# Pooled attention followed by eight experts on one core: chunk counts and weight maxima in the experts' PSUM banks as soon as they are ready, more slots for the weight loads, lists filled behind the first keys

## The chip, the cores and the metric

The kernel runs on one core of a Trainium2 chip. The metric is the device time of one execution in microseconds; the time before is the median of three runs. The engines are named as in the profile: PE (TensorE matmul), PEld (its weight loads), DVE (VectorE), ACT (ScalarE), POOL (GpSimd), SP (SyncE, which here only issues DMAs).

## The reference, cut to what matters

Four batches of 12288 queries attend to 768 keys each (keys and values are the same, a 4x4 mean pool of kv times a 128x128 matrix). The 49152 result rows are the tokens of a mixture of eight experts: each token goes to the one expert with the largest gate logit.

```python
kv_pool = kv.reshape(B, H // r, r, W // r, r, C).mean(axis=(2, 4))
k = v = kv_pool.reshape(B, -1, C) @ w_sr                  # 4 x 768 x 128
a = softmax(scale * (q @ k.transpose(0, 2, 1)))
x = (a @ v).reshape(B * S, D)                             # 49152 x 128
...
logits = x @ w_gate; e_idx = np.argmax(logits, axis=1)
gate_w = softmax(logits)[np.arange(N), e_idx]; eom = sigmoid(x @ w_output_gate)
for e in range(E):
    h = np.maximum(x[mask] @ w1[e], 0.0)                  # w1: 128 x 1024
    out[mask] = gate_w[mask, None] * eom[mask, e, None] * (h @ w2[e])
```

## The kernel before

**Work.** Float32 operands are split into two float16 halves, so each product is three float16 matmuls. 512 queries are a *group* (96 of them, number i); four groups are a *chunk* (24, number c). Nearly all tokens of a chunk have the same favourite expert, so the whole chunk is run through that expert, and the few other tokens are scattered to lists in DRAM (`scr`) and computed at the end, 128 per tile.

**Order of the work.** The main loop steps over i = 0 to 104, and each step over eight *slots* s. In a slot the work of several groups stands side by side: scores and softmax of group i (`qk`, on even slots, block j = s/2), value products of group i-1 (`pv`, in slot 5), gate logits of group i-2, and from i = 8 on (`MOE_LAG`) the expert of group i-8 (`moe_h`, `moe_y`: one block f of 128 hidden units per slot). PE, POOL and SP run exactly in the order in which this loop writes the instructions; DVE and ACT are ordered by the scheduler, which may pull an instruction ahead of earlier written ones. `with behind():` ties a DVE instruction behind the latest one that was marked (`mark["dve"]`: the score maximum or the latest `HL`).

**One slot of the expert.** PE makes H (three matmuls), ACT writes HH = relu(H) in float16, DVE writes HL = max(H,0) - HH, PE uses HH and HL for Y some slots later. H, the value product U, the logits `lg` and their transposes `lT` share one ring of three PSUM banks, `psH`: a new tile waits until the third last one has been read by ACT and DVE. Scores S have their own ring of two double banks, `psA`; columns 384 to 511 of each bank are free beside S's 384 columns.

**Routing.** When the logits of a chunk are there (step 4c+5), `routing(c)` runs as a generator, one stage per slot: maximum, one-hot (`oh`), sums per partition (`oh16`), then two small matmuls that count each expert's tokens in all and before each partition, then the favourite expert `ei`, then the indices, and 16 indirect DMAs on POOL that write `scr`. Before, the two count matmuls are put on a list `hooks`; the next `qk` with j in `HJ` (0 or 1; for the first steps not before (7, 0), `H0`) takes them off and writes the result into the free columns of its S.

**Weights.** `w_load(c)` reads `ei` on SP and loads the favourite's w1 and w2 (512 KB each). For the first six chunks (`NDW`) the float32 weights are then halved here by `w_split`, begun `WD` slots after the load: `w_power` takes the largest magnitude (four DVE reductions of 128x512), turns it round with two PE transposes (through `hooks` again, except c = 0), and gets a power of two; then ACT, DVE and POOL write the halves. From step `BK0` on, every `BKD` steps, `w_bank(e)` does the same for one of the eight experts, `BKW` slots after its load, and writes the halves to DRAM (`wbank`), where chunks 6 to 23 load them ready made.

**Lists.** `fill` sets the lists' 3.3 MB to a neutral row. Before, it begins at step 8 and issues one of eight DMAs every third slot (`FS`); a scatter waits until all are issued (`FILLED`).

Of the kernel before, what the change touches and what calls it, by code (L numbers as in the profile page):

```python
# [53 lines left out]
class Cfg:  # L54
# [12 lines left out]
    R3 = 2  # L67
    RG = 1
    RSEQ = (1, 2, 1, 1)
    FS = 3  # L70
    HJ = (0, 1)
    H0 = (7, 0)
    LC = 4
    WD = 4
    NDW = 6
    BK0, BKD, BKW = 11, 2, 8
    WT = 1
    QL, QT, QN = 0, 2, 6
    QP0, QPA = 4, 3
# [9 lines left out]
def body(ctx, tc, q, kv, w_sr, w_gate, w_og, w1, w2, out, cfg=Cfg):  # L89
# [61 lines left out]
    def largest(m, ps):  # L151

        dve.tensor_reduce(out=m, in_=ps, op=ALU.max, axis=AX.X)
        dve.tensor_scalar(m, m, 2.0 ** -100, None, op0=ALU.max)
# [195 lines left out]
        dve.tensor_tensor(qf[:, 1, :], ps, qf[:, 0, :], op=ALU.subtract)  # L350
        QS[i] = qT

    hooks = []
    spare = {"n": 0}

    def qk(i, j):

        K2 = KVT[i // GPB][0]
        KH, KL = K2[:, 0, :], K2[:, 1, :]
        c, g = divmod(i, CG)  # L360
        es = QM[c][:, 2, g:g + 1]
        if j == 0:
            PTt[i] = wk.tile([P, 2 * NKB, GT], F16, tag="PT", bufs=2, name=f"PT{i}")
            if g == 0:
                SUMS[c] = rt.tile([P, CB], F32, tag="SUM", bufs=4, name=f"SUM{c}")
        S = psA.tile([P, 2, 512], F32, tag="A", name=f"S{i}_{j}")
        if hooks and (j in cfg.HJ if i >= MOE_LAG else (i, j) >= cfg.H0):
            hooks.pop()(S)
        m = i - MOE_LAG - 1
        scale = moe_turn(m, j - 2, S) if j >= 2 and m >= 0 else None  # L370
        qh, ql = QS[i][:, j, :], QS[i][:, GB + j, :]
        for h in range(2):
            pe.matmul(S[:, h, 0:384], qh, KH[:, ts(h, 384)], start=True, stop=False)  # L373
        for h in range(2):
            pe.matmul(S[:, h, 0:384], qh, KL[:, ts(h, 384)], start=False, stop=False)  # L375
        for h in range(2):
            pe.matmul(S[:, h, 0:384], ql, KH[:, ts(h, 384)], start=False, stop=True)  # L377
        nm = wk.tile([P, 2], F32, tag="nm", bufs=4, name=f"nm{i}_{j}")
        with after(mark.get("nm")):
            dve.tensor_reduce(out=nm[:, 0:1], in_=S[:, :, 0:384], op=ALU.max, axis=AX.XY, negate=True)  # L380
# [3 lines left out]
        act.activation(pr.rearrange("p (a k) -> p a k", a=2), S[:, :, 0:384], AF.Exp,  # L384
                       bias=nm[:, 1:2], scale=es, accum_out=SUMS[c][:, bl:bl + 1])
# [87 lines left out]
    def routing(c):  # L473
# [27 lines left out]
        with nc.allow_low_precision("counts up to CB"):  # L501
            dve.tensor_reduce(out=oh16, in_=ohT, op=ALU.add, axis=AX.X)
        yield
        ps = []

        def counts(S):
            pe.matmul(S[:, 0, 384:384 + E], ones16, oh16, start=True, stop=True)
            pe.matmul(S[:, 1, 384:384 + E], tri16, oh16, start=True, stop=True)
            ps.append(S)

        if c == NCK - 1:
            for _ in range(cfg.LC):
                yield
            counts(psA.tile([P, 2, 512], F32, tag="A", name=f"cps{c}"))
        else:
            hooks.append(counts)
        while not ps:
            yield
        cnt = T("cnt", [P, 2, E])
        dve.tensor_copy(cnt, ps[0][:, :, 384:384 + E])  # L520
        yield
        cm = T("cm", [P, 4])
        dve.tensor_reduce(out=cm[:, 0:1], in_=cnt[:, 0, :], op=ALU.max, axis=AX.X)
# [56 lines left out]
        for n, t0, b in ((1, tok0, CT * c), (2, row0, 2 * CT * c), (3, row0, 2 * CT * c + GB)):  # L580
            pool.tensor_scalar(rw[:, :, n:n + 1], t0.unsqueeze(2), 1.0, float(b), op0=ALU.mult, op1=ALU.add)
        yield
        while not FILLED:
            yield
        SCT.add(c)
        for bl in range(CB):
            spare["n"] += 1
# [31 lines left out]
                     in_=w2[e, :, :].rearrange("o (k p) d -> p (o k) d", p=P))  # L619
        return t  # L620

    def w_power(t, nm, hook, x=""):

        m = kvp.tile([P, 8], F32, tag="wm" + x, name=f"wm{nm}")
        m4 = kvp.tile([P, 2, 2], F32, tag="wm4" + x, name=f"wm4{nm}")
        mb = kvp.tile([P, 2, P], F32, tag="wmb" + x, bufs=1, name=f"wmb{nm}")
        for y in range(2):
            for n in range(2):
                dve.tensor_reduce(out=m4[:, y, n:n + 1], in_=t[:, n, ts(y, 512)], op=ALU.max, axis=AX.X,
                                  apply_absolute_value=True)  # L630
            yield
        dve.tensor_tensor(m[:, 0:2], m4[:, 0, :], m4[:, 1, :], op=ALU.max)
        dve.tensor_copy(mb, m[:, 0:2].unsqueeze(2).to_broadcast([P, 2, P]))
        for _ in range(cfg.WT):
            yield
        ps = []

        def turn(S):
            for n in range(2):
                pe.transpose(S[:, n, 384:512], mb[:, n, :], ident)  # L640
            ps.append(S)

        if hook:
            hooks.append(turn)
        else:
            turn(psA.tile([P, 2, 512], F32, tag="A", name=f"wps{nm}"))
        while not ps:
            yield
        largest(m[:, 0:2], ps[0][:, :, 384:512])
# [27 lines left out]
    def w_bank(e):  # L677
# [83 lines left out]
    def fill():  # L761

        f = wk.tile([P, FR, RW], F32, tag="o", name="fill")
        pool.memset(f, 0.0)
        pool.memset(f[:, :, 1:2], BIG)
        pool.memset(f[:, :, 3:4], float(GB))
        yield
        for e in range(E):
            sp.dma_start(out=scr[e * REG:(e + 1) * REG, :].rearrange("(p a b) r -> p a (b r)", p=P, b=FR),
                         in_=f.rearrange("p b r -> p (b r)").unsqueeze(1).to_broadcast([P, REG // P // FR, FR * RW]))  # L770
# [122 lines left out]
    with tc.manual_schedule(engines={pool.engine, sp.engine, pe.engine}):  # L893
# [44 lines left out]
        for i in range(NG + MOE_LAG + 1):  # L938
# [140 lines left out]
```

## Time and profile before

| | |
|---|---|
| median of three runs | 2064.8 us (2062.18 to 2068.03) |
| profiled execution, time | 2063.95 us |
| its span (first to last instruction) | 2062.2 us |
| PE busy | 1916.5 us, 93% |
| DVE busy | 1608.1 us, 78% |
| ACT busy | 1381.6 us, 67% |
| POOL busy | 1156.2 us, 56% |
| mean granted TensorE clock | 0.989 |

Besides the page, the profile is read through views: a table of busy times by stretch of time, a list of who waited for whom, and the instructions in order of time. A time in these views counts from the span's first instruction. In a row of the table by stretch the numbers are: the stretch, its length, then busy us and count for PE, PEld, DVE, ACT and POOL, the granted clock, the DMA share and GB/s. In a row of the instructions in order of time they are: start, duration, engine, line, operation, and in brackets the idle time before it and what ended it. Step i begins with the first matmul of S for group i, j = 0; by that, step 8 begins at 132.4 us, 11 at 195.6, 15 at 289.5, 19 at 384.9, 23 at 477.4, 27 at 571.8, 31 at 660.4, and steps 41 to 44 last from 862.6 to 940.9.

### The profile page before, as it was taken

The numbers are of one execution on the slowest core, as the hardware profiler recorded it, in microseconds if no ns is written. First come the engines' busy times: TensorE is split into PE (matmuls) and PEld (weight loads), VectorE is DVE, ScalarE is ACT, GpSimd is POOL, SyncE is SP. The second block draws the span as 40 slices with busy tenths as digits, with TensorE's granted clock in tenths as the row PEclk, the third lists the DMA queues.
The fourth block names the chain that finished last, engine by engine and source line by source line (L and its number), as shares of the span: only waits on it lengthen the run. The fifth ranks groups of instructions, "written<-read, shape, count | busy, mean of one in ns | idle before, by whom it ended". The sixth has DMA issues, their size and how long they took to land. (4 is left out here: it accounts for less than half of the span.)

```text
span 2062.2 us, 30671 instructions
## 1 busy us (share of the span) xinstructions
PE 1916.5 (93%) x9789; PEld 976.6 (47%) x9789; DVE 1608.1 (78%) x3296; ACT 1381.6 (67%) x2470; POOL 1156.2 (56%) x995
## 2 busy tenths in 40 slices
PE   4878989798999999999999999999999999999997
PEld 2544444343444544444544544445445445445444
DVE  6788798988878778788687687787787787786673
ACT  3766767676767676776777766776776776776653
POOL 1543667666566765654656756645645645646531
PEclk9989999999999999999999999999999999999999
DMA  6979989888897887888889997977977977877712
GB/s 182 179 153 248 218 205 220 196 176 190 185 206 178 186 189 154 163 157 165 163 185 200 186 193 135 179 166 141 184 158 144 179 160 152 172 153 147 144 54 66
DMA packets 898898, 351.07 MB, mean 170 GB/s; under 512 B 822240, under 2 KB 840801, under 8 KB 898736
## 3 DMA queue, kind: packets, MB, share of 16 engines
q1 hardware_dynamic: 885824, 348.63, 81.1%
q0 software_dynamic: 12480, 0.40, 0.5%
q8 instruction: 78, 1.28, 0.3%
q14 instruction: 84, 0.69, 0.1%
q10 hardware_dynamic: 432, 0.07, 0.0%
HBM read 86.19 MB, written 62.91 MB: 72 GB/s over the span
## 5 line engine op out<-in xcount | busy, mean ns | idle before, releaser
L391 POOL TENSOR_TENSOR ph<-pr,ph 128x768 f16<-128x768 f32 x384 | 632.3, 1647 | 709.6 <-ACT ph L390 424.0
L711 DVE SCALAR_TENSOR_TENSOR HL<-H,HH 128x512 f16<-128x512 f32 x768 | 526.3, 686 | 115.8 <-ACT HH L710 103.2
L710 ACT ACTIVATE HH<-H 128x512 f16<-128x512 f32 x768 | 452.4, 590 | 213.9 <-PE H L707 211.0
L384 ACT ACTIVATE pr<-S,nm,qm 128x768 f32<-128x768 f32 x384 | 380.3, 990 | 202.3 <-DVE nm L381 163.5
L588 POOL DMA_INDIRECT scr<-rw,idx x384 | 384.3, 1001 | 93.8 <-issue 80.8
L418 PE MATMUL U<-PT,V 128*128 128x512 f16 (+1 forms) x1854 | 393.4, 367 | 33.1 <-DVE HL L711 27.9
L380 DVE TENSOR_REDUCE nm<-S 128x1 f32<-128x768 f32 x384 | 364.7, 950 | 49.8 <-PE S L377 49.2
L705 PE MATMUL H<-U,w 128*128 128x512 f16 x768 | 293.0, 381 | 31.5 <-DVE U L423 15.1
L390 ACT ACTIVATE ph<-pr 128x768 f16<-128x768 f32 x368 | 309.3, 840 | 3.6 <-issue 2.1
L721 PE MATMUL Y<-HH,w 128*128 128x512 f16 x768 | 292.3, 381 | 4.7 <-ACT ys L726 4.0
L418 PEld LDWEIGHTS <-V 128*128 128x128 f16 x1854 | 181.5, 98 | 238.8 <-issue 45.6
L723 PE MATMUL Y<-HL,w 128*128 128x512 f16 x768 | 292.2, 381 | 2.3 <-DVE HL L711 2.3
L706 PE MATMUL H<-U,w 128*128 128x512 f16 x768 | 292.8, 381 | 0.0
L707 PE MATMUL H<-U,w 128*128 128x512 f16 x768 | 292.8, 381 | 0.0
L722 PE MATMUL Y<-HH,w 128*128 128x512 f16 x768 | 292.1, 380 | 0.0
L373 PE MATMUL S<-K,qT 128*128 128x384 f16 x768 | 189.5, 329 | 9.9 <-ACT pr L384 4.7
L375 PE MATMUL S<-K,qT 128*128 128x384 f16 x768 | 189.5, 329 | 0.0
L377 PE MATMUL S<-K,qT 128*128 128x384 f16 x768 | 189.4, 329 | 0.0
L423 DVE SCALAR_TENSOR_TENSOR U<-U,U 128x512 f16<-128x512 f32 x96 | 64.8, 675 | 127.1 <-ACT U L422 127.1
L422 ACT ACTIVATE U<-U 128x512 f16<-128x512 f32 x96 | 56.8, 592 | 120.4 <-PE U L418 120.3
L706 PEld LDWEIGHTS <-w 128*128 128x128 f16 x768 | 75.3, 98 | 104.2 <-issue 42.3
L722 PEld LDWEIGHTS <-w 128*128 128x128 f16 x768 | 75.3, 98 | 96.5 <-issue 10.3
(222 smaller groups left out, 2185.2 us busy)
## 6 DMA issues: line engine op xcount, KB each, us to landing
kvs<-in_kv_dram SPq DMA_DIRECT2D x96, 256.0 KB
q<-in_q_dram SPq DMA_DIRECT2D x96, 256.0 KB
urows<-uT SPq DMA_DIRECT2D x96, 256.0 KB
out_dram<-o SPq DMA_DIRECT2D x96, 256.0 KB
w<-wbank SPq DMA_DIRECT2D x36, 512.0 KB
wb<-in_moe_w_dram SPq DMA_DIRECT2D x16, 512.0 KB
wbank<-wbo SPq DMA_DIRECT2D x16, 512.0 KB
PT<-ph SPq DMA_TRANSPOSE x384
```

The costliest lines, as they stand in the source:

```text
L380: dve.tensor_reduce(out=nm[:, 0:1], in_=S[:, :, 0:384], op=ALU.max, axis=AX.XY, negate=True)
L384: act.activation(pr.rearrange("p (a k) -> p a k", a=2), S[:, :, 0:384], AF.Exp, bias=nm[:, 1:2], scale=es, accum_out=SUMS[c][:, bl:bl + 1])
L390: act.activation(ph[:, 0, :], pr, AF.Copy)
L391: pool.tensor_tensor(ph[:, 1, :], pr, ph[:, 0, :], op=ALU.subtract)
L418: pe.matmul(PVP[i][:, cols], ops[n][0], ops[n][1][:, cols], start=(n == 0), stop=(n == len(ops) - 1))
L588: ins = pool.indirect_dma_start(out=scr, out_offset=bass.IndirectOffsetOnAxis(ap=idx[:, bl:bl + 1], axis=0), in_=rw[:, bl, :], in_offset=None,
L705: pe.matmul(H, w1h[:, ts(f, P)], UH, start=True, stop=False)
L706: pe.matmul(H, w1h[:, ts(f, P)], UL, start=False, stop=False)
L707: pe.matmul(H, w1l[:, ts(f, P)], UH, start=False, stop=True)
L710: act.activation(HH, H, AF.Relu)
L711: mark["dve"] = dve.scalar_tensor_tensor(HL, H, 0.0, HH, op0=ALU.max, op1=ALU.subtract)
L722: pe.matmul(Y, w2l[:, ts(f, P)], HH, start=False, stop=False)
```

## The change

Five things are changed together.

1. The two count matmuls and the transposes of the weights' maxima no longer go through `hooks` into the free columns of S. They take a bank of the ring `psH`, and are issued one slot after `oh16` (counts), `WT` = 1 slot after the maxima (chunk weights) or `BKT` = 3 slots after them (experts' bank).
2. The four reductions of `w_power` are one per slot instead of two, and each is tied `behind()` the latest marked DVE instruction.
3. `w_split` begins six slots after its load instead of four (`WD`).
4. The experts' banks begin at step 9 instead of 11 (`BK0`), and wait 14 slots instead of 8 for their loads (`BKW`).
5. `fill` is issued at once behind the first keys' and the first three query loads, and no scatter waits for it any more.

```diff
-    FS = 3
-    HJ = (0, 1)
-    H0 = (7, 0)
     LC = 4
-    WD = 4
+    WD = 6
     NDW = 6
-    BK0, BKD, BKW = 11, 2, 8
+    BK0, BKD = 9, 2
+    BKW, BKT = 14, 3
...
     def qk(i, j):
...
-        if hooks and (j in cfg.HJ if i >= MOE_LAG else (i, j) >= cfg.H0):
-            hooks.pop()(S)
...
     def routing(c):
...
-        def counts(S):
-            pe.matmul(S[:, 0, 384:384 + E], ones16, oh16, start=True, stop=True)
-            pe.matmul(S[:, 1, 384:384 + E], tri16, oh16, start=True, stop=True)
-            ps.append(S)
-
-        if c == NCK - 1:
-            for _ in range(cfg.LC):
-                yield
-            counts(psA.tile([P, 2, 512], F32, tag="A", name=f"cps{c}"))
-        else:
-            hooks.append(counts)
-        while not ps:
+        for _ in range(cfg.LC if c == NCK - 1 else 1):
             yield
+        ps = psH.tile([P, GT], F32, tag="H", name=f"cps{c}")
+        pe.matmul(ps[:, 0:E], ones16, oh16, start=True, stop=True)
+        pe.matmul(ps[:, E:2 * E], tri16, oh16, start=True, stop=True)
         cnt = T("cnt", [P, 2, E])
...
-        while not FILLED:
-            yield
         SCT.add(c)
...
     def w_power(t, nm, wt, x=""):
...
-        for y in range(2):
-            for n in range(2):
-                dve.tensor_reduce(out=m4[:, y, n:n + 1], in_=t[:, n, ts(y, 512)], op=ALU.max, ...)
-            yield
+        for n in range(2):
+            for y in range(2):
+                with behind():
+                    dve.tensor_reduce(out=m4[:, y, n:n + 1], in_=t[:, n, ts(y, 512)], op=ALU.max, ...)
+                yield
...
-        for _ in range(cfg.WT):
+        for _ in range(wt):
             yield
...
+        ps = psH.tile([P, GT], F32, tag="H", name=f"wps{nm}")
+        for n in range(2):
+            pe.transpose(ps[:, ts(n, P)], mb[:, n, :], ident)
+        largest(m[:, 0:2], ps[:, 0:2 * P].rearrange("p (n x) -> p n x", n=2))
+        yield
...
         for i in (1, 2):
             q_load(i)
+        fill()
         q_power(0, 0, 1)
```

**What stands where, before and after.** In the rows below a name carries the group or chunk and then the block (S41_3 is block 3 of group 41's scores, HL33_6 block 6 of group 33's hidden units), with the tile's running number behind it. Lines are those of the kernel before and of the changed one, each in its own count.

SP at the first weight load: `ei0` is read from SBUF (TENSOR_LOAD), then chunk 0's two weight tensors (`wr0`) are loaded; `PT` are the transposes of the probabilities. Before:

```order
L401 DMA_TRANSPOSE PT7_1142<-ph7_0_1157 128x12x128
L334 DMA_TRANSPOSE qT9_1196<-q29_1193 128x8x128
L604 TENSOR_LOAD ei0_1172
L604 ISA x2
L617 ISA
L617 DMA wr0_1207<-in_moe_w1_dram 128x1024
L618 ISA
L618 DMA wr0_1207<-in_moe_w2_dram 128x8x128
L401 DMA_TRANSPOSE PT7_1142<-ph7_1_1186 128x12x128
```

After:

```order
L396 DMA_TRANSPOSE PT5_883<-ph5_3_1005 128x12x128
L291 DMA q12_1061<-in_q_dram 128x512
L587 TENSOR_LOAD ei0_1040
L587 ISA x2
L600 ISA
L600 DMA wr0_1072<-in_moe_w1_dram 128x1024
L601 ISA
L601 DMA wr0_1072<-in_moe_w2_dram 128x8x128
L396 DMA_TRANSPOSE PT6_1042<-ph6_0_1055 128x12x128
```

The load has moved up by a little over one step: it stands ahead of group 6's first transpose instead of behind group 7's first.

DVE at the end of step 10 and the start of step 11: `wm41` are the four reductions of chunk 1's weights, `wm4b0` those of expert 0's bank, `U29` the value product of group 9, `nm` score maxima. Before:

```order
L741 TENSOR_TENSOR o1_1938<-S10_2_1937,msw0_1346 128x256
L629 TENSOR_REDUCE wm41_2042<-wr1_1904 128x1 x2
L332 SCALAR_TENSOR_TENSOR q215_2661<-q15_1578,qm3_1160,q215_2661 128x512
L629 TENSOR_REDUCE wm41_2042<-wr1_1904 128x1 x2
L423 SCALAR_TENSOR_TENSOR U29_2001<-U9_1982,U29_2001 128x512
L380 TENSOR_REDUCE nm10_3_2021<-S10_3_2012 128x1
L711 SCALAR_TENSOR_TENSOR HL2_6_2035<-H2_6_2030,HH2_6_2034 128x512
```

After:

```order
L716 TENSOR_TENSOR o1_2013<-S10_2_2012,msw0_1341 128x256
L686 SCALAR_TENSOR_TENSOR HL2_5_2052<-H2_5_2047,HH2_5_2051 128x512
L613 TENSOR_REDUCE wm41_2084<-wr1_1875 128x1
L330 SCALAR_TENSOR_TENSOR q215_2746<-q15_1633,qm3_1244,q215_2746 128x512
L418 SCALAR_TENSOR_TENSOR U29_2077<-U9_2058,U29_2077 128x512
L375 TENSOR_REDUCE nm10_3_2099<-S10_3_2090 128x1
L376 TENSOR_SCALAR nm10_3_2099<-nm10_3_2099,qm2_652 128x1
L686 SCALAR_TENSOR_TENSOR HL2_6_2113<-H2_6_2108,HH2_6_2112 128x512
L613 TENSOR_REDUCE wm41_2084<-wr1_1875 128x1
L716 TENSOR_TENSOR o1_2013<-S10_3_2090,msw0_1341 128x256
L686 SCALAR_TENSOR_TENSOR HL2_7_2128<-H2_7_2123,HH2_7_2127 128x512
L613 TENSOR_REDUCE wm4b0_2136<-wb0_1637 128x1
```

One reduction instead of four stands ahead of `U29`; the others are spread between the `HL`.

DVE at the end of step 41, where PE has written the value product U40 and S41_3 (`scl9`, `cnt9` to `x19` are routing of chunk 9). Before:

```order
L541 SCALAR_TENSOR_TENSOR z9_10170<-z9_10170,sume9_9919 128x16
L542 SCALAR_TENSOR_TENSOR z9_10170<-se9_10166,z9_10170 128x16
L544 RECIPROCAL scl9_10189<-z9_10170 128x16
L423 SCALAR_TENSOR_TENSOR U240_10013<-U40_9994,U240_10013 128x512
L380 TENSOR_REDUCE nm41_3_10026<-S41_3_10017 128x1
L381 TENSOR_SCALAR nm41_3_10026<-nm41_3_10026,qm10_8405 128x1
L711 SCALAR_TENSOR_TENSOR HL33_6_10040<-H33_6_10035,HH33_6_10039 128x512
L741 TENSOR_TENSOR o32_9952<-S41_3_10017,msc8_9229 128x256
```

After:

```order
L529 RECIPROCAL scl9_10148<-z9_10109 128x16
L505 COPY cnt9_10042<-cps9_10039 128x16
L508 TENSOR_REDUCE cm9_10073<-cnt9_10042 128x1
L549 SCALAR_TENSOR_TENSOR st9_10210<-cnt9_10042,ebase_101 128x8
L510 SCALAR_TENSOR_TENSOR ce9_10075<-cnt9_10042,cm9_10073,w8_95 128x8
L551 TENSOR_TENSOR x19_10212<-x09_10174,st9_10210 128x128
L418 SCALAR_TENSOR_TENSOR U240_10035<-U40_10016,U240_10035 128x512
L375 TENSOR_REDUCE nm41_3_10053<-S41_3_10044 128x1
L511 TENSOR_REDUCE cm9_10073<-ce9_10075 128x1
L552 TENSOR_TENSOR x19_10212<-x19_10212,oh9_9969 128x128
L376 TENSOR_SCALAR nm41_3_10053<-nm41_3_10053,qm10_8435 128x1
L686 SCALAR_TENSOR_TENSOR HL33_6_10067<-H33_6_10062,HH33_6_10066 128x512
```

Before, the counts' followers come behind `nm42_0` and `HL34_0` in step 42; now the first five of them stand ahead of `U240`. On PE the two count matmuls stand between U40 and S41_3 (before: ahead of S42_0), and in the ring `psH` their tile stands between U40 and H33_6, so that H33_7 now takes the bank of U40, which H34_0 took before.

More of the change, by code (lines that the diff above doesn't have):

```diff
@@ L351, in q_prep @@
         QS[i] = qT
-    hooks = []
     spare = {"n": 0}
@@ L503, in routing @@
         yield
-        ps = []
-        def counts(S):
-            pe.matmul(S[:, 0, 384:384 + E], ones16, oh16, start=True, stop=True)
-            pe.matmul(S[:, 1, 384:384 + E], tri16, oh16, start=True, stop=True)
-            ps.append(S)
-        if c == NCK - 1:
-            for _ in range(cfg.LC):
-                yield
-            counts(psA.tile([P, 2, 512], F32, tag="A", name=f"cps{c}"))
-        else:
-            hooks.append(counts)
-        while not ps:
+        for _ in range(cfg.LC if c == NCK - 1 else 1):
             yield
+        ps = psH.tile([P, GT], F32, tag="H", name=f"cps{c}")
+        pe.matmul(ps[:, 0:E], ones16, oh16, start=True, stop=True)
+        pe.matmul(ps[:, E:2 * E], tri16, oh16, start=True, stop=True)
         cnt = T("cnt", [P, 2, E])
-        dve.tensor_copy(cnt, ps[0][:, :, 384:384 + E])
+        dve.tensor_copy(cnt, ps[:, 0:2 * E].rearrange("p (x e) -> p x e", x=2))
         yield
@@ L620, in w_raw, with w_power @@
         return t
-    def w_power(t, nm, hook, x=""):
+    def w_power(t, nm, wt, x=""):
         m = kvp.tile([P, 8], F32, tag="wm" + x, name=f"wm{nm}")
@@ L626, in w_power @@
         mb = kvp.tile([P, 2, P], F32, tag="wmb" + x, bufs=1, name=f"wmb{nm}")
-        for y in range(2):
-            for n in range(2):
-                dve.tensor_reduce(out=m4[:, y, n:n + 1], in_=t[:, n, ts(y, 512)], op=ALU.max, axis=AX.X,
-                                  apply_absolute_value=True)
-            yield
+        for n in range(2):
+            for y in range(2):
+                with behind():
+                    dve.tensor_reduce(out=m4[:, y, n:n + 1], in_=t[:, n, ts(y, 512)], op=ALU.max, axis=AX.X,
+                                      apply_absolute_value=True)
+                yield
         dve.tensor_tensor(m[:, 0:2], m4[:, 0, :], m4[:, 1, :], op=ALU.max)
         dve.tensor_copy(mb, m[:, 0:2].unsqueeze(2).to_broadcast([P, 2, P]))
-        for _ in range(cfg.WT):
+        for _ in range(wt):
             yield
[L636 to L649, printed above, removed]
+        ps = psH.tile([P, GT], F32, tag="H", name=f"wps{nm}")
[3 more added lines that the diff above has]
+        yield
         powers(m[:, 2:4], m[:, 4:6], m[:, 0:2])
@@ L655, in w_split @@
         t = WT[c]
-        m = yield from w_power(t, f"{c}", att and c)
+        m = yield from w_power(t, f"{c}", cfg.WT)
         MSC[c] = msc = rt.tile([P, CB], F32, tag="msw", bufs=4, name=f"msw{c}")
@@ L685, in w_bank @@
             yield
-        m = yield from w_power(t, f"b{e}", True, "_b")
+        m = yield from w_power(t, f"b{e}", cfg.BKT, "_b")
         dve.tensor_copy(fac[:, e:e + 1], m[:, 6:7])
@@ L766, in fill @@
         pool.memset(f[:, :, 3:4], float(GB))
-        yield
         for e in range(E):
@@ L770, in fill @@
                          in_=f.rearrange("p b r -> p (b r)").unsqueeze(1).to_broadcast([P, REG // P // FR, FR * RW]))
-            yield
-        FILLED.append(True)
-    FILLED = []
     def tail_prep():
@@ L909, in body @@
         tix, tgen = [], []
-        filler, begun = None, False
+        begun = False
         bk, nbk = [], 0
@@ L946, in body @@
                 rc = None
-            if i == MOE_LAG:
-                filler = fill()
             for s in range(8):
-                if filler and (8 * i + s) % cfg.FS == 0 and next(filler, 1) == 1:
-                    filler = None
                 if s == 0 and 0 <= ri < NG:
```

## The prediction

> **What bounds the kernel now.** I read the page first: which engine is full, and in which part of the span it is not.
>
> ```profile
> PE 1916.5 (93%) x9789; PEld 976.6 (47%) x9789; DVE 1608.1 (78%) x3296; ACT 1381.6 (67%) x2470; POOL 1156.2 (56%) x995
> PE   4878989798999999999999999999999999999997
> DVE  6788798988878778788687687787787787786673
> ```
>
> PE is the bound, and from the eleventh slice on (516 us) it stays at nine tenths or more. Most of its missing 146 us (2062.2 - 1916.5) lie ahead of that. So the table by stretch came second, cut where groups 8, 11, 15, 19, 23 and 27 begin, with one late chunk (steps 41 to 44) as the measure.
>
> ```profile
> 132.40:195.60 63.20, 60.45 (x290) 28.99 (x289) 48.08 (x103) 40.22 (x71) 22.27 (x18) 0.93 0.90 198
> 195.60:289.50 93.90, 83.73 (x407) 41.31 (x406) 76.77 (x154) 64.33 (x116) 59.95 (x50) 0.95 1.04 236
> 289.50:384.90 95.40, 81.65 (x409) 40.83 (x408) 82.86 (x165) 64.44 (x116) 65.11 (x57) 0.98 0.88 197
> 384.90:477.40 92.50, 80.62 (x409) 40.41 (x407) 79.19 (x172) 64.93 (x117) 60.10 (x53) 1.00 0.85 185
> 477.40:571.80 94.40, 82.97 (x403) 40.35 (x401) 80.62 (x171) 64.18 (x113) 52.23 (x44) 0.96 0.87 185
> 571.80:660.40 88.60, 81.13 (x402) 40.26 (x400) 74.55 (x147) 62.31 (x113) 58.56 (x50) 0.98 0.87 193
> 862.60:940.90 78.30, 77.19 (x395) 38.96 (x394) 61.53 (x123) 55.16 (x99) 42.89 (x36) 1.00 0.86 162
> ```
>
> Four steps cost 78.3 us late and 92.5 to 95.4 us in the four stretches from 195.6 to 571.8, which hold the experts' banks and the chunks' own weights: 376.2 us against 313.2, 63 us lost, and 10.3 more in the stretch behind. DVE does 76.8 to 82.9 us there against 61.5 late, so it is nearly a second bound. Third came the list of waits from 132 to 660 us, and in it those of PE, and of DVE and ACT for a DMA.
>
> ```profile
> PE H L705 <- DVE U L423: 15.1, 6, 4.6
> PE H L705 <- DVE HL L711: 13.4, 18, 2.0
> PE U L418 <- DVE HL L711: 12.8, 8, 2.8
> PE wps L640 <- DVE wmb L633: 9.3, 1, 9.3
> DVE wm4b L629 <- DMA wb<-in_moe_w_dram: 9.0, 6, 4.1
> DVE wm L629 <- DMA wr<-in_moe_w_dram: 4.1, 4, 1.8
> ACT q L331 <- DMA qT<-q: 7.9, 2, 4.6
> ```
>
> PE waits 41.3 us for banks of `psH` that DVE has not yet read (15.1+13.4+12.8), and DVE in turn stands 13.1 us before weights that have not landed. How the two hang together is seen in order of time:
>
> ```profile
> 194.76 0.43 DVE L741 TENSOR_TENSOR o<-S,msw 128x256 f32<-128x256 f32 x1 [4.54 <-ACT pr L384]
> 196.81 1.28 DVE L629 TENSOR_REDUCE wm<-wr 128x1 f32<-128x512 f32 x2 [1.62 <-DMA wr<-in_moe_w_dram]
> 198.69 1.28 DVE L629 TENSOR_REDUCE wm<-wr 128x1 f32<-128x512 f32 x2
> 199.88 0.68 DVE L423 SCALAR_TENSOR_TENSOR U<-U,U 128x512 f16<-128x512 f32 x1
> 200.62 0.58 PE L705 MATMUL H<-U,w 128*128 128x512 f16 x1 [3.89 <-DVE U L423]
> 214.58 0.69 DVE L629 TENSOR_REDUCE wm4b<-wb 128x1 f32<-128x512 f32 x1 [4.14 <-DMA wb<-in_moe_w_dram]
> ```
>
> Four reductions of chunk 1's weights, with their wait, stand ahead of U; PE idles 3.89 us until U is out of its bank. At 214.58 the same engine waits 4.14 us for the bank's weights.
>
> **The change part by part.** The sum is made against the profiled execution, 2063.95 us: its span of 2062.2 and 1.75 around it. The median is 0.85 us above it.
>
> *Start (steps 5 to 8).* The single wait of 9.3 us is PE's for the turn of chunk 0's maxima. Counts, favourite and weight load move up by about one step, so the wait as such should go. But what comes in its place is DVE:
>
> ```profile
> 111.90:122.00 10.10, 8.60 (x65) 6.02 (x65) 10.10 (x27) 6.34 (x11) 6.56 (x4) 1.00 0.85 151
> 122.00:136.00 14.00, 3.27 (x15) 1.56 (x13) 10.81 (x26) 5.57 (x8) 3.98 (x6) 0.69 0.97 218
> ```
>
> DVE is busy without a gap from 111.9 to 122 us, and 10.81 of the next 14.0 us. Its work is only put in another order, so the first H cannot come earlier than DVE's 3.2 idle us allow. Part of PE's 9.3 us will be spread over steps 6 and 7 as waits for DVE. SP reads `ei0` earlier too, and group 6's transposes queue behind that; DVE writes `ei0` ahead of that group's second maximum, so I cost it nothing; were DVE late, SP would hold back `PT` by that much. I take -3 us, and -1 for the granted clock, 0.69 in that stretch; ends 0 and -9.3.
>
> [...]
>
> *Lists.* The eight DMAs, first and last issued at 149.6 and 213.9 us in the last row here, move to the place behind the third query load.
>
> ```profile
> 15.00:20.00 5.00, 3.08 (x10) 1.69 (x8) 4.86 (x11) 1.61 (x6) 0.00 (x0) 1.00 1.05 388
> 25.00:30.00 5.00, 2.34 (x6) 1.37 (x6) 2.61 (x7) 0.83 (x3) 0.00 (x0) 1.00 0.01 2
> 30.00:35.00 5.00, 1.97 (x6) 0.67 (x6) 3.11 (x14) 1.40 (x3) 0.00 (x0) 1.00 0.00 0
> 35.00:40.00 5.00, 4.03 (x15) 1.70 (x13) 3.92 (x9) 1.08 (x2) 0.93 (x1) 1.00 0.00 0
> scr<-fill SPq DMA_DIRECT2D x8, 400.0 KB
> L769 SPq DMA_DIRECT2D scr<-fill x8: 587/882/1692, 149.6 to 213.9; - x8
> ```
>
> 3.2 MB at the 388 GB/s of 15..20 us are 8.4 us, and eight issues of 0.88 us are 7.1 us on SP. The DMA engines are idle from 25 to 40 us, so all of it lies beside the making of the keys: 0. Behind it in the queue stand two query loads (0.5 MB, 1.4 us) that are used steps later; if the cover were gone, the first transposes would slip by the 8.4 us at most. What leaves the stretch from 132 to 289 us, where the DMA share is 0.90 and 1.04, is counted next.
>
> *Waits for weights and the order on DVE (steps 8 to 30).* The load of chunk weights is used two slots later (`WD`) and issued three or four slots earlier, that of the bank is used six slots later, a slot being some 2.4 us (78.3 us over 32 slots); the longest waits are 1.8 and 4.1 us. So the 13.1 us of DVE's waits for weights should go, and the 7.9 us of ACT's wait for a query transpose too, since these lie where the lists are written: 21.0 us. All of this is upstream of the 41.3 us that PE waits for DVE. The new order (one reduction between two `HL`) takes away delays of up to 2.6 us in front of U (1.28 and 1.28 above), but DVE's work remains: step 11 still holds the chunk's maxima and a bank's. I take -20 us for the four stretches, as the named DMA waits say, -1 for steps 8 to 10, and -4 for steps 27 to 30, where the last bank ends about a step earlier. Ends: 0 if DVE is as late as now, and 376.2 less 319.4 (its busy sum 76.77+82.86+79.19+80.62) = -56.8 if it never idles.
>
> *Turns of the maxima in `psH`.* 14 pairs of transposes now stand at a fixed place on PE. For chunks 1 to 5 one slot lies between the copy on DVE and the turn; with one long DVE instruction (0.68 us, as U above) late ahead of the copy, PE waits that long: 5 x 0.7 = +3.5, already taken off in choosing -20 rather than more. The bank's three slots cover it.
>
> *Counts in `psH`, all 24 chunks.* No more matmuls than before. DVE's followers of the counts come ahead of U's evacuation, and H33_7 waits for just that bank.
>
> ```profile
> 879.89 0.63 DVE L423 SCALAR_TENSOR_TENSOR U<-U,U 128x512 f16<-128x512 f32 x1
> 880.44 0.94 DVE L380 TENSOR_REDUCE nm<-S 128x1 f32<-128x768 f32 x1
> 880.47 0.38 PE L705 MATMUL H<-U,w 128*128 128x512 f16 x1
> 894.59 1.67 PE L418 MATMUL U<-PT,V 128*128 128x512 f16 x7 [1.11 <-DVE HL L711]
> L523 DVE TENSOR_REDUCE cm<-cnt x24: 151/161/163, 116.7 to 1974.0; 128x1 f32<-128x8 f32 x24
> L564 DVE SCALAR_TENSOR_TENSOR st<-cnt,ebase x24: 156/160/1552, 116.7 to 1974.1; 128x8 f32<-128x8 f32 x24
> L525 DVE SCALAR_TENSOR_TENSOR ce<-cnt,cm,w x24: 214/218/1618, 118.9 to 1974.3; 128x8 f32<-128x8 f32 x24
> L520 DVE COPY cnt<-S x23: 145/174/175, 116.5 to 1912.1; 128x16 f32<-128x16 f32 x23
> L566 DVE TENSOR_TENSOR x<-x,st 128x128 f32<-128x128 f32 x24 | 9.8, 410 | 0.0
> ```
>
> Now U ends at 880.52, and H33_7 (the matmul at 880.47) need not wait, as it takes another bank. Five instructions ahead (0.17+0.16+0.16+0.22+0.41 = 1.12 us) put U's end at 881.64: H33_7 waits 1.17 us. In exchange the counts' followers leave step 42, where PE waits 1.11 us at 894.59 for an `HL` that DVE is late with. DVE works nearly without a gap from one place to the other, and a later PE waits less at the second; so the chunk should come out about even. I take +0.2 us for each of 15 late chunks: +3; ends +17.6 (15 x 1.17, nothing given back) and -16.7 (15 x 1.11, the late wait gone and no new one).
>
> Sum: -4 -20 -1 -4 +3 = -26; 2063.95 - 26 = 2038 us, and 2039 from the median. I say 2038.
>
> **The rivals.**
>
> *A: DVE gives nothing back, about 2060 us.* If the crowded steps are held by DVE's work and not by its waits, the removed 21.0 us are lost again to the chunk and bank maxima that still meet in step 11 and in each fourth one. For it: DVE busy 82.86 of 95.4 us. Against: DVE's waits of 4.54 and 1.62 us come directly before PE's 3.89. Only the start's -4 would stay.
>
> *B: DVE runs almost through, about 2008 us.* Each crowded chunk comes to 82.5 us, three above DVE's mean of 79.9: 376.2 - 330 = -46, with -4 -1 -8 +3 for the rest: -56. For it: with counts earlier and reductions spread, no DVE instruction waits for a transfer. Against: DVE also waits for ACT's halves, which the change does not touch.
>
> *C: the ring is one bank short, about 2080 us, slower.* The place is H33_7 behind U in every chunk. The maxima in the rows of L564 and L525 show instructions of 0.16 and 0.22 us that took 1.4 us longer now and then; if one of the five ahead of U does so in each chunk, the wait is 2.6 us, and with nothing given back 23 x 2.6 = 59 us. Against the -29 of the other parts that makes +30, 2094; with half of it given back, 2064. It decides from 29/23 = 1.3 us lost per chunk on. I put 2080. Against it: DVE's slack in step 42.
>
> [...]
>
> **How the numbers follow.** Chances: my forecast (2020 to 2052) 0.62, A 0.14, B 0.14, C 0.10. About 0.3%, 6 us, is what a measurement of this kernel can tell from no change. Faster takes my forecast, B and a third of A (0.62+0.14+0.05 = 0.81), same 0.10, slower 0.09. The range leaves out half of B below and C above: 2009 to 2060.
>
> **What would show it.** Right: the lists' eight issues stand at 20 to 28 us and the first score matmul comes no later than before; no wait of DVE's L613 for `wr` or `wb`; the stretches of steps 11 to 26 come to 86 to 91 us each; PE's wait for `wmb` at the start falls below 5 us; in late chunks a wait of H (L680) for U (L418) near 1 us and a shorter one before U. Wrong: crowded chunks still above 92 us (A), or late chunks above 79.5 us where they were 78.3 (C). Most of the forecast hangs on the -20: if PE's waits for DVE there do not shrink with DVE's waits for transfers, it is wrong.

## The result, and the profile after

The changed kernel takes 2113.0 us (median, 2112.39 to 2113.93), the kernel before 2064.28 us on the same chip: ratio 1.0234, 95% interval 1.0217 to 1.0252. It is slower by 49 us where 26 us less were forecast. The page of the changed kernel, and its table by stretch for steps 11 to 26 (four rows of four steps) and for the single steps 41 to 43:

```profile
PE 1937.4 (92%) x9789; PEld 983.1 (47%) x9789; DVE 1602.0 (76%) x3296; ACT 1380.3 (65%) x2470; POOL 1168.5 (55%) x995
```

```profile
198.20:294.50 96.30, 83.46 (x407) 41.15 (x406) 83.45 (x168) 65.79 (x118) 56.01 (x46) 0.96 0.96 215
294.50:390.90 96.40, 83.37 (x408) 41.67 (x407) 83.24 (x164) 65.06 (x116) 60.33 (x51) 0.96 0.88 197
390.90:487.20 96.30, 84.71 (x408) 42.07 (x407) 84.32 (x177) 66.66 (x119) 57.38 (x49) 0.95 0.82 180
487.20:579.10 91.90, 82.02 (x401) 40.52 (x400) 80.94 (x165) 63.74 (x111) 49.58 (x41) 0.96 0.82 175
872.30:892.30 20.00, 20.00 (x108) 10.51 (x107) 17.72 (x41) 11.86 (x22) 6.57 (x4) 1.00 0.75 145
892.30:914.10 21.80, 19.46 (x98) 9.46 (x97) 17.08 (x38) 14.93 (x27) 9.86 (x10) 1.00 0.82 172
914.10:934.60 20.50, 19.43 (x98) 9.50 (x97) 13.52 (x26) 14.77 (x27) 14.47 (x12) 1.00 0.88 143
```

The late chunk costs 81.3 us instead of 78.3; the loss lies in steps 42 (21.8, it was 20.4) and 43 (20.5, it was 19.0). DVE does no more work than before (busy 1602.0 us, it was 1608.1). By stretches, from the first S of one step to that of the next named one, in every kernel of this study (us):

| kernel | ratio to before | steps 0-7 | 8-10 | 11-26 | 27-30 | 31-94 |
|---|---|---|---|---|---|---|
| before | | 98.7 | 63.2 | 376.2 | 88.6 | 1266.6 |
| changed | 1.0234 | 99.9 | 64.2 | 380.9 | 87.1 | 1309.8 |
| e1 counts back | 0.9999 | 99.8 | 65.0 | 370.7 | 91.5 | 1266.2 |
| e2 counts alone, late chunks | 1.0177 | 99.9 | 62.7 | 379.3 | 88.5 | 1305.4 |
| e4 counts three slots later | 0.9942 | 95.1 | 66.0 | 364.8 | 91.1 | 1261.6 |
| e5 four query buffers | 1.0137 | 98.1 | 65.2 | 374.1 | 87.1 | 1297.4 |
| e6 three slots to the turn | 1.0241 | 93.4 | 73.4 | 379.4 | 90.9 | 1305.3 |
| e7 changed, POOL only fills | | 89.7 | 63.4 | 355.5 | 78.2 | 1250.3 |
| e8 e4 with `WD` = 4 | 1.0065 | 101.6 | 63.7 | 395.9 | 86.5 | 1261.1 |
| e9 before, POOL only fills | | 92.0 | 62.5 | 350.9 | 82.4 | 1236.9 |
| e10 e4 with e5 | 0.9897 | 96.9 | 66.4 | 364.6 | 91.2 | 1254.5 |
| e11 e10, counts a slot earlier | 1.0150 | 99.5 | 68.1 | 386.6 | 88.9 | 1286.0 |
| e12 e10, counts a slot later | 0.9979 | 98.4 | 64.7 | 374.8 | 87.3 | 1262.9 |
| e13 before, with e10's counts and buffers | 0.9937 | 99.1 | 62.9 | 377.9 | 83.1 | 1254.6 |

(The 1287 and 1330 us that the expectations name for steps 31 to 95 are these 1266.6 and 1309.8 with 20 us for step 95.) So 43.2 of the 49 us are lost in the late chunks, where I had put +3: 26.8 in the 16 steps 4k+2 (as step 42), 13.0 in the steps 4k+3 (as step 43).

Beside e1, e2, e4, e6 and e10 to e13 the kernel before takes 2082 to 2083 us, beside the others 2064, so every ratio here is to the kernel before run beside it on the same chip. e7 and e9 leave out part of the result and ran once each; they have no ratio.

What happens there is seen in order of time, steps 41 to 43 of the changed kernel; only the instructions that matter are kept:

```profile
889.65 0.11 DVE L505 COPY cnt<-cps 128x16 f32<-128x16 f32 x1
...
894.96 1.65 POOL L386 TENSOR_TENSOR ph<-pr,ph 128x768 f16<-128x768 f32 x1 [6.60 <-ACT ph L385]
895.14 1.49 DVE L561 TENSOR_TENSOR nd<-nd,cnt 128x8 f32<-128x8 f32 x1
896.75 0.95 DVE L375 TENSOR_REDUCE nm<-S 128x1 f32<-128x768 f32 x1
897.87 0.68 DVE L686 SCALAR_TENSOR_TENSOR HL<-H,HH 128x512 f16<-128x512 f32 x1
...
898.60 0.38 PE L680 MATMUL H<-U,w 128*128 128x512 f16 x1 [1.22 <-DVE HL L686]
...
900.39 0.38 PE L680 MATMUL H<-U,w 128*128 128x512 f16 x1 [0.98 <-DVE HL L686]
...
912.19 0.75 DVE L330 SCALAR_TENSOR_TENSOR q<-q,qm,q 128x512 f16<-128x512 f32 x1 [3.70 <-ACT q L329]
...
920.60 0.38 PE L680 MATMUL H<-U,w 128*128 128x512 f16 x1 [0.64 <-DVE HL L686]
```

Between the counts' copy (889.65) and 896.75 DVE runs all of the followers among its other work, and the last but one of them, the product `nd` of 128x8, takes 1.49 us: it starts 0.18 us after POOL's subtraction and ends just behind it, at 896.63. The row maximum `nm` and the `HL` that PE needs for its bank stand behind it: PE waits 1.22 and then 0.98 us. Twenty us later DVE stands 3.70 us behind ACT's query half, and one step on PE waits again. The same product, first in the kernel before, then in the changed one (minimum, median and maximum in ns):

```profile
L576 DVE TENSOR_TENSOR nd<-nd,cnt x24: 151/154/296, 124.2 to 1977.5; 128x8 f32<-128x8 f32 x24
```

```profile
L561 DVE TENSOR_TENSOR nd<-nd,cnt x24: 150/1486/1615, 115.0 to 2026.4; 128x8 f32<-128x8 f32 x24
```

In at least half of the chunks it now takes ten times as long; before, it never took more than 0.3 us. By the order of time, one of the counts' followers takes 1.49 to 1.69 us within 0.7 to 3.2 us behind the start of each of the 16 steps 4k+2 from 34 to 94: this product in 13, the instruction ahead of it in two, `msc` in one. And the list of waits of the changed kernel for the whole span has two rows, the first of which stood at 8.6 us before and the second at nothing:

```profile
ACT q L329 <- DMA qT<-q: 42.8, 17, 5.1
DVE q L330 <- ACT q L329: 62.3, 35, 5.8
```

ACT's query half stands up to 5.1 us behind a transposing DMA that still reads the third of three buffers (`q2`); with a fourth one (e5) ACT's list has no such row. DVE stands behind ACT, up to 5.8 us at once, with everything that comes after the query half in its order.

In the table by stretch, steps 31 to 94 as a whole (kernel before, then changed):

```profile
660.40:1927.00 1266.60, 1241.72 (x6340) 627.74 (x6339) 990.49 (x1966) 887.49 (x1591) 735.95 (x626) 1.00 0.84 167
```

```profile
666.20:1976.00 1309.80, 1258.86 (x6340) 631.42 (x6339) 974.63 (x1967) 884.98 (x1594) 742.82 (x626) 0.99 0.81 162
```

PE's idle time grows from 24.9 to 50.9 us, and its busy time, for the same 6340 groups of instructions, by 17.1 us more.

In the crowded steps the list of PE's waits from 132 to 666 us reads:

```profile
PE wps L622 <- DVE nm L376: 19.9, 4, 5.1
PE H L680 <- DVE HL L686: 14.1, 17, 1.7
...
PE lg L432 <- DVE HL L686: 4.6, 3, 2.5
PE wpsb L622 <- DVE cnt L505: 3.2, 4, 1.7
PE H L680 <- DVE U L418: 3.2, 5, 0.9
PE wps L622 <- DVE wmb L617: 2.9, 1, 2.9
```

Two rows of the same list before, beside those that the prediction shows:

```profile
PE lg L437 <- DVE HL L711: 2.4, 5, 0.8
PE S L640 <- DVE wmb L153: 1.8, 1, 1.8
```

The waits for banks of `psH` that DVE has not read, 43.7 us before (the prediction's 41.3 and the 2.4 of `lg`), are 21.9 (14.1+4.6+3.2). The 9.3 us of the list before are chunk 0's turn, which ends with step 7. The turns of the maxima behind it, 1.8 us before, are 26.0 (19.9+3.2+2.9), 5 us at a time for the weights of chunks 1 to 4:

```profile
208.51 1.63 POOL L386 TENSOR_TENSOR ph<-pr,ph 128x768 f16<-128x768 f32 x1 [1.36 <-ACT ph L385]
208.65 1.50 DVE L616 TENSOR_TENSOR wm<-wm 128x2 f32<-128x2 f32 x1
...
210.08 0.94 DVE L375 TENSOR_REDUCE nm<-S 128x1 f32<-128x768 f32 x1
...
210.95 0.46 DVE L617 COPY wmb<-wm 128x256 f32<-128x256 f32 x1
...
211.56 0.66 PE L622 MATMUL wps<-ident,wmb 128*128 128x128 f32 x2 [5.05 <-DVE nm L376]
```

A product of 128x2 takes 1.50 us beside POOL, a row maximum follows, then the copy, and PE, which has the turn at a fixed place, stands 5.05 us.

### The profile page after: what moved, and what is told of

The parts are those of the page before. It is cut to its first block, busy times and chain, and to the rows that moved or that the text cites. A ratio compares the mean times of both kernels' runs of the same rounds, so it can differ in the third digit from the quotient of the medians.

```text
span 2111.1 us, 30691 instructions
## 1 busy us (share of the span) xinstructions
PE 1937.4 (92%) x9789; PEld 983.1 (47%) x9789; DVE 1602.0 (76%) x3296; ACT 1380.3 (65%) x2470; POOL 1168.5 (55%) x995
## 5 line engine op out<-in xcount | busy, mean ns | idle before, releaser
L375 DVE TENSOR_REDUCE nm<-S 128x1 f32<-128x768 f32 x384 | 364.8, 950 | 51.5 <-PE S L372 50.7
L697 PEld LDWEIGHTS <-w 128*128 128x128 f16 x768 | 75.6, 98 | 104.1 <-issue 20.5
```

What stands on the lines that cost most here:

```text
L697: pe.matmul(Y, w2l[:, ts(f, P)], HH, start=False, stop=False)
```

## The experiments

Theory 1: the counts' earlier followers cost the late chunks, by their place on DVE (1a), by the fourth user of `psH` (1b, rival C of the forecast), or through GpSimd's stalls (1c). Theory 2: another part of the change does.

**e1, the counts undone.** The changed kernel with the counts back in S's free columns:

```diff
-        ps = psH.tile([P, GT], F32, tag="H", name=f"cps{c}")
...
+            hooks.append(counts)
```

> The changed kernel with one part undone: the chunk counts stand again in the free columns of S tiles, and so come about three slots later; turns of the maxima, slots for the weights and the early lists stay as changed. Theory 1 (the counts alone cost the late chunks): steps 31 to 95 take 1287 us again instead of 1330, and the whole 2113 - 43 = 2070 us, or less if the crowded chunks gain too. Theory 2 (the late loss comes from another part, for instance the lists or the weights' order): 2113 us within 6, and steps 31 to 95 stay at 1330.

Ratio 0.9999 (0.9989 to 1.0008); steps 31 to 94 take 1266.2 us. Theory 1: the whole late loss belongs to the counts. The rest of the change together is worth nothing: -5.5 us in steps 11 to 26, given back around them.

**e2, the counts alone.** The kernel before, with the counts in `psH` from chunk 7 on:

```diff
-            hooks.append(counts)
+            if c < 7: hooks.append(counts)
+            else: ps = psH.tile([P, GT], F32, tag="H", name=f"cps{c}")
```

> The kernel before with only the counts moved, and only from chunk 7 on: in a psH bank, one slot after the one-hot sums; everything up to step 30 stays as before. Theory 1: 17 chunks lose 2.7 to 2.9 us each, 46 to 49 us in all, so about 2064 + 47 = 2111 us. Theory 2: 2064 us within 6.

Ratio 1.0177 (1.0160 to 1.0194), +38.8 us in steps 31 to 94. Theory 1, though 8 us short of the 47 expected.

**e4, the same banks at another time.** The changed kernel with one number altered:

```diff
-        for _ in range(cfg.LC if c == NCK - 1 else 1):
+        for _ in range(cfg.LC if c == NCK - 1 else 4):
```

> The changed kernel with the counts still in psH banks, but taken three slots later (four instead of one after the one-hot sums), where the kernel before took them. Tells the two mechanisms of theory 1 apart. Theory 1a (the time of the followers on DVE: ahead of U's evacuation and of the row maxima of step 4k+2 they make the maxima, ACT's exponentials and HL late): the waits in step 4k+2 fall from 2.3 us to about 1.1, step 4k+3 loses its 1.07, steps 31 to 95 take 1287 to 1297 us, the whole about 2072. Theory 1b (a fourth user of the three psH banks): the banks are still shared, so steps 31 to 95 stay at 1320 to 1330 and the whole at 2105 to 2113 us.

Ratio 0.9942 (0.9925 to 0.9958): faster than the kernel before. Steps 31 to 94 take 1261.6 us, 5 less than before, with the counts in `psH` all the same. That is some 5 us below the range of 1a too: step 42 takes 19.6 us where the kernel before took 20.4. So 1b falls: at this place a fourth user of the ring costs nothing, and the time of the followers decides. e7 below keeps the counts' tile at its early place in the ring, and there step 42 has no wait either.

**e6, more slots ahead of the turns.** The changed kernel with `WT` = 3:

```diff
-    WT = 1
+    WT = 3
```

> The changed kernel with three slots instead of one between the copy of a chunk's weight maxima on DVE and its turn on PE (chunks 0 to 5). Theory: PE stood 19.9 us at four of these turns and 2.9 at a fifth because the copy was 5 us late on DVE; with two slots (4.8 us) more these waits nearly go, 15 to 20 us less in steps 11 to 30: about 2095 us. Rival: DVE's work sets these steps, the wait moves to the next H or U, and the time stays at 2113 within 6.

Ratio 1.0241 (1.0224 to 1.0258): the rival. One row of PE's waits from step 11 to 26 shows why:

```profile
PE H L682 <- POOL w L647: 10.7, 4, 3.8
```

PE no longer waits for the copy of the chunks' maxima, but the halves of the weights, which POOL writes last, come as much later, and H waits for them.

**e5, a fourth buffer for the query halves.** The changed kernel with

```diff
-        q2 = wk.tile([P, 2, GT], F16, tag="q2", bufs=3, name=f"q2{i}")
+        q2 = wk.tile([P, 2, GT], F16, tag="q2", bufs=4, name=f"q2{i}")
```

> The changed kernel with four buffers instead of three for the query halves. Tests the largest new row of waits: ACT's q stands 42.8 us behind query transposes that still read the third buffer, and DVE's q 62.3 us behind ACT. Theory: DVE's 3.7 us behind it make step 4k+3 lose its 1.07 us; without it 8 to 10 of the late chunks gain about 1.1 us, so 2101 to 2105 us, on a chip as for the first run of the change (ratio 1.018 to 1.020). Rival: only the order on DVE counts, the wait is a consequence of it; 2113 us within 6 (ratio 1.020 to 1.026).

Ratio 1.0137 (1.0120 to 1.0154), 20 us less and more than either theory gave. Step 43 takes 19.0 us again and step 42 is unchanged (21.8). The wait shrinks to

```profile
DVE q L330 <- ACT q L329: 19.3, 32, 0.7
```

with at most 0.7 us at once. The want of a fourth buffer accounts for 12.4 us of the 43.2, and for 6.8 us in steps 11 to 26.

**e7 and e9, POOL without its reads.** Both kernels with GpSimd's subtraction replaced:

```diff
-        pool.tensor_tensor(ph[:, 1, :], pr, ph[:, 0, :], op=ALU.subtract)
+        pool.memset(ph[:, 1, :], 0.0)
```

> The changed kernel with GpSimd's subtraction, the low half of the probabilities, left out: a fill with zeros stands in its place, which writes the same tile and reads nothing. The sums keep their count of instructions. Theory 1a (order of DVE's work alone): DVE's instructions of 0.15 to 0.2 us that took 1.4 to 1.5 us beside GpSimd's subtraction (1.50 us for a 128x2 product, 1.49 us for a 128x8 one) take 0.15 to 0.2 us, but steps 31 to 95 still lose 20 us or more against the kernel before with the same edit. Theory 1c (the stalls make the loss): the loss between the two kernels with this edit is below 10 us in steps 31 to 95. If the stalls have nothing to do with GpSimd, the long instructions stay.

> The kernel before with the same edit, GpSimd's subtraction replaced by a fill with zeros (the low half of the probabilities is left out); the measure for the run of the changed kernel with it. Theory: the stalled DVE instructions (1.68 us for a 128x4 product, 2.14 us for a query half of 0.74) take their usual time, the wait of 1.11 us in each step 4k+2 shrinks to 0.5 us or less, steps 31 to 95 take 1265 to 1280 us instead of 1287. If the stalls have nothing to do with GpSimd: 1287 us and the same long instructions.

One run each: 2007.7 us changed, 1995.1 us before. The product of 128x8 in e7:

```profile
L561 DVE TENSOR_TENSOR nd<-nd,cnt x24: 144/166/169, 106.3 to 1921.2; 128x8 f32<-128x8 f32 x24
```

It takes its usual time again. Step 42 takes 19.0 us without a wait in both kernels, so the 1.11 us of the kernel before come from stalls too (there the 128x4 product of `qm` takes 1.67 us in the median, in e9 0.22); that kernel gains more than expected. Between the two, 13.4 us remain in steps 31 to 94, 11.4 of them in steps 4k+3. This agrees with the 12.4 us of the query buffer: DVE stands 66.7 us behind ACT's query halves in e7 and 0.7 us in e9. This lies between the bounds of 1a and 1c, and neither alone is right: the order brings the work ahead of `nm` and `HL`, the stall makes it long. Without the one (e4) or the other (e7) step 42 loses nothing against the kernel before. The fill is also shorter than the subtraction (0.74 against 1.64 us), and none of the 24 products of e7 begins during a fill. The scan of 128x128, which reads two tiles as well, tells the two apart; first the kernel before, then e9:

```profile
L560 DVE TENSOR_TENSOR_SCAN x<-run,oh x24: 409/1771/1822, 107.5 to 1971.5; 128x128 f32<-128x128 f32 x24
```

```profile
L560 DVE TENSOR_TENSOR_SCAN x<-run,oh x24: 405/416/420, 101.2 to 1902.5; 128x128 f32<-128x128 f32 x24
```

Before, 18 of the 24 scans begin during a subtraction; in e9, eight begin during a fill, and none takes longer than 0.42 us. So it is not the length alone: a fill that is running does not hold them. It does hold another instruction: in e7 this `qm`, a product of one tile with a factor per partition, begins 13 times during a fill, ends with it, and takes 0.34 to 0.63 us instead of 0.22.

Nor does the subtraction hold every instruction. Of the changed kernel's scans, 20 of 24 begin during one, and the median is 1.81 us. Of its `HL`, which take H from PSUM and only HH from SBUF, 122 of 768 begin during one, and none takes more than 0.69 us. What decides which instruction is held the runs do not show.

**e8, the slots for the weights undone.** In e4 PE waits from step 11 to 26 for the chunk weights and for the counts' bank:

```profile
PE H L682 <- POOL w L647: 11.9, 4, 3.0
PE lg L432 <- DVE cnt L505: 9.9, 4, 2.9
PE H L680 <- ACT w L645: 4.2, 4, 1.1
```

So e4 with

```diff
-    WD = 6
+    WD = 4
```

> The changed kernel with the counts three slots later (still in psH) and four instead of six slots for a chunk's weights. With the counts late, PE waits 11.9 us for POOL's and 4.2 us for ACT's part of the chunk weights in steps 11 to 26, since all follows the counts. Theory: taking back the two slots (4.8 us) removes most of these 16 us and brings back at most 4 us of DVE's wait for the load: 10 us faster than with six slots, ratio to the kernel before 0.988 to 0.991. Rival: DVE's work sets these steps, ratio 0.994 within 0.002.

Ratio 1.0065 (1.0048 to 1.0082): both wrong. Steps 11 to 26 take 395.9 us, 31 more. The waits for the weights are gone, and DVE's are back:

```profile
PE H L680 <- DVE HL L686: 19.1, 10, 3.1
PE wps L622 <- DVE wmb L617: 9.1, 4, 2.5
```

Two slots earlier the chunk's reductions presumably meet more of DVE's other work; which meeting does it was not tried apart.

**e10 to e12, both causes taken away.** The changed kernel with four query buffers and the counts four slots after the one-hot sums (e10), three (e11) or five (e12):

```diff
-        for _ in range(cfg.LC if c == NCK - 1 else 1):
+        for _ in range(cfg.LC if c == NCK - 1 else 4):
...
-tag="q2", bufs=3
+tag="q2", bufs=4
```

> The changed kernel with both causes of the late loss taken away: the counts three slots later (still in psH) and four buffers for the query halves. With the late counts alone the ratio was 0.9942, and ACT still stood 22.3 us behind query transposes. Theory (two causes that add up): steps 31 to 95 gain another 4 us or so in the steps 4k+3, the crowded ones up to 6: ratio 0.990 to 0.992. Rival: the rest of the query waits is hidden once the counts are late; ratio 0.994 within 0.002.

> The same with the counts two slots later instead of three. Their copy then stands on DVE ahead of the last HL of step 4k+1 and most followers ahead of the row maxima of step 4k+2. Theory 1a: with each slot earlier more of the followers, and a stall behind GpSimd, fall ahead of these maxima; slower than the one above by 5 to 25 us. Rival (only the very first place, ahead of U, is bad): within 4 us of it.

> The same with the counts four slots later. Theory: in the late chunks the place is no worse, within 6 us in steps 31 to 95; in steps 11 to 26 the chunk weights, for which PE already waits 16 us with three slots, come a slot of 2.4 us later for chunks 1 to 5, so up to 12 us slower. Rival: the wait of lg for the counts' bank (9.9 us there) goes instead, and the time is the same or 5 us better.

e10: ratio 0.9897 (0.9882 to 0.9911), the fastest kernel here that computes the whole result. The forecast was right in the sum and not in its parts: against e4, steps 31 to 94 gain 7.1 us instead of 4, and steps 11 to 26 only 0.2 instead of up to 6. e11: 1.0150 (1.0130 to 1.0170), over 50 us slower than e10 where 5 to 25 were expected, 31.5 of them in steps 31 to 94 and 22.0 in steps 11 to 26; the way is 1a's, the size is not. e12: 0.9979 (0.9970 to 0.9988). One slot of 2.4 us makes 2.5% between e11 and e10. In e11 a follower of the counts that takes 0.2 us otherwise takes 1.70 us ahead of `nm` and `HL`, and PE waits 0.95 and 0.91 us. In e10 the order of time shows where the stall has gone:

```profile
878.08 0.69 DVE L686 SCALAR_TENSOR_TENSOR HL<-H,HH 128x512 f16<-128x512 f32 x1
...
879.02 1.75 DVE L551 TENSOR_TENSOR x<-x,st 128x128 f32<-128x128 f32 x1
```

It is there still, 1.75 us long beside a subtraction that POOL began at 878.91, but directly behind an `HL` that has just freed PE's bank; PE then waits 0.33 us in step 42, where it waited 1.11 us in the kernel before. In e12 steps 31 to 94 lose 8.4 us against e10 (2 above the bound that I gave) and steps 11 to 26 10.2 us.

**e13, only the counts and the buffers.** The kernel before with e10's two numbers, its weights and lists as they were:

```diff
-            hooks.append(counts)
+            H = psH.tile([P, GT], F32, tag="H", name=f"cps{c}")
...
-tag="q2", bufs=3
+tag="q2", bufs=4
```

> The kernel before with only two things of the fastest version: from chunk 2 on the counts in psH banks, three slots later than in the change (four after the one-hot sums), and four buffers for the query halves. Weights, turns of the maxima, experts' banks and lists stay as before. Tells what the change's other parts are worth in the fastest version (ratio 0.9897). Theory: the 12 us of steps 31 to 95 come from the counts and the fourth buffer, and the 11.6 us of steps 11 to 26 from the weights' parts; so this one saves the 12 us alone, ratio 0.993 to 0.996. Rival: the weights' parts give nothing, and the gain in steps 11 to 26 comes from the counts too; ratio 0.988 to 0.991.

Ratio 0.9937 (0.9920 to 0.9954), as expected: steps 31 to 94 gain 12.0 us, 11 to 26 nothing (+1.7), 27 to 30 5.5 us. The change's other parts are thus worth 0.4% in the fastest version, and only there.

## Why the prediction was wrong, point by point

- **What bounds the kernel**: held. PE is the bound, and DVE's order decides what PE waits for.
- **Start, -4**: +1.2 us. PE's wait for the turn fell to 2.6 us, but its waits for S stand at 9.7 us, as the list from 80 to 135 us shows:

```profile
PE S L368 <- ACT pr L379: 9.7, 7, 4.3
PE wps L622 <- DVE wmb L617: 2.6, 1, 2.6
```

  Before, they stood at 1.7 us. The working said that DVE would spread the wait; it did so entirely: ACT, which reads S, stands 10.0 us of that time behind DVE's row maxima. The granted clock did rise, from 0.69 in 122 to 136 us to 1.00 in 122 to 134 us, and the stretch still gained nothing (from 134 to 138 us it was 0.60). With the counts later it takes 95.1 and 96.9 us (e4, e10).
- **Lists, 0**: held. All eight are issued from 19.2 to 26.3 us, and the first S comes at 34.1 us (33.7 before).
- **Steps 8 to 10, -1, and 27 to 30, -4**: +1.0 and -1.5 us.
- **DVE's waits for weights, 13.1 us**: they are gone, as said. ACT's 7.9 us for a query transpose were not due to the lists: 8.6 us are left there, and e5, with a fourth buffer, has no such row in its list of ACT's waits.
- **Steps 11 to 26, -20**: +4.7 us. The step that failed is "all of this is upstream of the 41.3 us that PE waits for DVE": half of these went (43.7 to 21.9 us with `lg`), and the turns took what was won (1.8 to 26.0 us). Even with the counts put right (e4, e10) the term is -11.4 and -11.6; the waits then stand at the halves of the weights, which come six slots after a load that itself follows the later counts. With four slots (e8) these waits go and others come. I had named nothing that is late next.
- **Turns, 0.7 us each**: 5 us each at four of five. I allowed for one long instruction of 0.68 us ahead of the copy. PE came to chunk 1's turn at 206.5 us, when DVE still had four of 0.68 us, the stalled product of 1.50 us and a row maximum to do. With the counts later (e1, e4) no turn has a wait in steps 11 to 26; the halves of the weights have 16.1 us in their place (11.9 for POOL's, 4.2 for ACT's, in both).
- **Counts, +3**: +43.2 us, the term that decides. I priced five followers at their medians (1.12 us) ahead of U, looked for the wait at H33_7, and let a later place give it back. The wait for U at H33_7 does not exist. In step 41 H33_7 begins while DVE's reading of U40 has yet to begin:

```profile
890.31 0.38 PE L680 MATMUL H<-U,w 128*128 128x512 f16 x1
890.42 0.68 DVE L418 SCALAR_TENSOR_TENSOR U<-U,U 128x512 f16<-128x512 f32 x1
```

  It is so in all 16 chunks of steps 31 to 94, and in steps 33 and 37 the same H waits 0.65 us for the copy of the counts (L505). So it does not take the bank of U40, as was said ahead of the prediction; by these waits it takes that of the counts. The followers did delay U, at no cost that shows in step 41; the loss came in the next step, where the rest of them, which had no term in the sum, stood ahead of `nm` and `HL`, one of them (`nd`) with a median that was no longer 154 but 1486 ns: the stall goes with the place of an instruction. The query halves, which the scheduler put elsewhere too, ran out of buffers; I had counted their one wait among the lists' and not asked what else it depends on.
- **Rival C** named the right direction and nearly the price (2.6 us per chunk at worst; steps 31 to 94 lost 2.7 for each of 16 chunks) and even quoted the stalled rows, with a chance of one in ten. That is luck in part: its mechanism, a ring one bank short at H33_7, is refuted by e4 and by the rows above, and in e9 the wait of 1.11 us in step 42 is gone with the ring as it was. "DVE's slack in step 42", which I held against it, is a mean over a step (17.1 of 21.8 us busy); the order inside the step used it up.

## What to carry to other kernels

The price of a small instruction is not its median: look at the maxima of its row (the 128x8 product: 154 ns in the median at the old place, 1486 at the new one), ask what it met there, and ask what it will meet at the new place. When work is moved earlier on an engine whose instructions wait in line (DVE stood 3.70 us behind one query half here), list what is then queued behind it (here the row maximum that ACT waits for, and the `HL` that frees PE's bank), and see which buffer ring the shifted neighbours run into. When a new place loses, try the neighbouring slots with everything else left alone: here one number moved the kernel from 1.5% slower to 1.0% faster.

## What the runs showed of the hardware that was not expected

**Half clock after short gaps.** In the table by stretch of the changed kernel, the same 5.9 us of steps 50 and 42, each from 6.1 us behind the step's start and with the waits of 1.2 and 0.98 us:

```profile
1061.00:1066.90 5.90, 4.70 (x16) 2.14 (x16) 4.93 (x11) 5.90 (x12) 1.64 (x1) 0.71 0.72 177
898.40:904.30 5.90, 4.58 (x23) 2.23 (x23) 5.14 (x12) 5.90 (x12) 1.64 (x1) 1.00 0.83 201
```

In step 50 the granted clock falls to 0.71 (0.50 from 1063.2 to 1066.6 us) and PE gets 16 groups of instructions done, in step 42 it stays at 1.00 and there are 23. Five matmuls then take 0.63 us instead of 0.38, and the step 23.2 instead of 21.8 us. Of the changed kernel's steps from 31 to 94, 13 have such a pair of waits and seven of these the half clock, 3.4 us each time; the kernel before has no half clock there. Together this is about 10 of the 17.1 us by which PE's busy time grew (7 x 1.4, an estimate). In the seven the half clock begins between 0.13 us ahead of and 0.70 us behind the end of the second wait, and the two waits make 2.2 to 2.5 us; in the other six they make 2.2 to 2.6 us, without it. So their length does not decide, and what does the runs do not show.

**ACT stops for something not traced.** In e1, e2, e4, e6 and e10 to e13 ACT stands behind step 94 for something that none of the traced engines releases, 8 to 22 us in all, as a row of e10's waits from 1908 us on shows:

```profile
ACT HH L685 <- remote: 16.6, 3, 12.8
```

The kernel before, the changed one, e5 and e8 have no such row there. The time from step 95 to the end of the span is 151 to 155 us in these eight and 135 to 137 us in the others, while the steps agree (e1 and the kernel before take 1266.2 and 1266.6 us for steps 31 to 94). It does not go with the chip: e5 and e8 without these waits and e10 to e12 with them ran on the same one. What it is stays open.
